# A memset moved behind three weight loads, the first eighth of a written instruction list put in a new order, and seven PSUM evictions on another engine

## The chip, the core and the metric

The kernel runs on one core of a Trainium2 chip. A core has TensorE (PE; its weight loads are shown as PEld), VectorE (DVE), ScalarE (ACT), GpSimd (POOL) and SyncE (SP), each with an in-order queue of its own, an on-chip memory (SBUF) and eight accumulator banks per partition (PSUM), into which only TensorE's products go. Transfers run on 16 DMA engines and are issued from SP, ACT or POOL. The metric is device time in microseconds (us) of one execution; lower is better.

## What is computed

Two stages follow each other. `q`, `k` and `v` have the shape (8, 8, 576, 64) (batch, head, token, dimension), `phi` has (8, 8, 576, 32); all inputs and the output are float32, the kernel computes on float16 operands with float32 accumulation.

```
a    = softmax(phi, over the 32 memory slots)
k_m  = einsum('bhsm,bhsd->bhmd', a, k);  v_m = einsum('bhsm,bhsd->bhmd', a, v)
attn = softmax(q @ k_m^T / 8);           o   = attn @ v_m
x    = o as (4608 tokens, 512)
out  = ((x @ w_a) * (x @ w_b)) @ w_out        # 512 -> 1536 -> 512
```

## The kernel before

**Work.** The eight batches go through the same steps. For a batch, phi is exponentiated (`exp_phi`, L301, ScalarE, in two halves `exp0` and `exp1` of two head pairs each); TensorE forms the sums over tokens of keys, values and a constant column that gives the softmax's denominator (batch 0: `sums`, L387, result pk, one half of the heads at a time; later batches: `kv_sums`, L333, result pkv); VectorE divides them (L396 and L397 for batch 0, `take_kv` L360 and L365 for the others); TensorE turns them (`transpose` L405, `kv_transpose` L373) and VectorE copies them back (L408, L374, the tile kvT, for batch 0 kept in vsum). VectorE turns the queries in 32x32 blocks (`q_transpose` L310, `q_transpose_half` L316). TensorE forms the scores (pscore, L422 and L452), ScalarE their exponentials E (L435, L465). A product with a block matrix of ones (pD, L475) gives the denominators; ScalarE takes Ln (L476) and Exp of its negative (L486), and a tensor_tensor (L240) multiplies into A, the normalised weights.

Instead of forming o, the kernel folds v_m into the weights: `fold` (L526, result pva) multiplies v_m by a slice of w_a or w_b, and `take_fold` (L558) casts the result from PSUM to the float16 tile vab. For batch 0 the first 512 columns are folded in halves of 256. The up-projections (`up_half`, L737) then multiply vab by A: pa is evicted to SBUF as a_sb (L741), pb is multiplied by a_sb on VectorE into ht (L744). Each is done for a batch, a block i of 128 of the 1536 hidden units, and one part of the tokens (288 tokens, for batch 1 320 or 256). The down-projection (L664 and the lines behind it) uses a seven-product scheme on 2x2 blocks, for which sums of tokens (h_sums, from ht) and of weights (w_sums) are formed (L240). From batch 5 on the up-projections use it too (L760).

**What sets the order.** A scheduler doesn't: the string `PLAN` lists every step, and each engine gets its instructions in that order. The letters that matter here: `wa0:256` issues the load of those columns of w_a on GpSimd's queue, and `k1`, `v1`, `p1`, `q1`, `o3` those of keys, values, phi and queries of a batch or a part of w_out; `M` is GpSimd's memset of the constant 1/16 into the tile of keys and values of the odd batches (L802); `O` makes the matrix of ones (memset on VectorE, L269, then two selects on GpSimd, L270 and L272); `F4` runs four matmuls of a zero tile as fill (pw, L229); `0ks1`, `0kt1`, `0vs1`, `0vt1` are the sums of keys or values and their turn for batch 0 and half 1; `0qt1` turns a query block; `0s1`, `0e1`, `0den11`, `0nr11` are scores, exponentials, denominators and normalisation; `0hv0b` and `0hx0b1` are a fold in halves and its cast, `0v1a` and `0x1a0` those of full width; `a1.2.0` and `b1.2.0` are the two up-projections of batch 1, block 2, token part 0; `h0.3` and `g0.3` are a sum of tokens on GpSimd or on VectorE, `T20` and `V00` a sum of weights on GpSimd or VectorE; `d3` takes three steps of the down-projection.

PSUM banks are handed out in order of last use; a fold, scores or pkv hold theirs until their eviction stands in the list. So a TensorE instruction can wait for the eviction, on VectorE or ScalarE, of what its bank held eight allocations earlier.

**Before the list.** The keys of batch 0 come as float32 in two halves, issued from SP and ACT (L185), and VectorE casts them (L235) behind a memset of its own (L233). GpSimd issues phi, queries and values of batch 0 (L149, L160, L155), then makes the identity for the transposes, then takes up the list.

**Which engine evicts.** In `up_half` ScalarE copies every pa. In `take_fold` the two halves g of a fold go to `first` and `second`: VectorE where true, ScalarE where false:

```
first, second = b == 0 and hi <= 512, b < 2
copies = [nc.vector.tensor_copy if x else nc.scalar.copy for x in (first, second)]
```

Of the kernel before, what the change touches and what calls it, by code (L numbers as in the profile page):

```python
# [22 lines left out]
1x1a0 1v0b F1 1x0b0 a0.4.0 1v0a 1x0a0 1qh10 a0.6.1 F1 a0.6.0 1qh00 1x0a1 1qh20 1sh0 1eh10 1eh00 1x0b1 wb512:1024 0v1b  # L23
0x1b0 1x1a1 q1.1 wb1024:1536 wa1024:1536 0x1b1 1v1b a0.5.1 1x1b1 1den10 1den00 b0.6.0 b0.5.1 o3 b0.4.0 1nr10 1nr00
a0.4.1 b0.4.1 a0.7.0 b0.6.1 1qh31 o4 a0.5.0 b0.5.0 1qh01 o0 1x1b0 1qh11 o1 a0.7.1 b0.7.1 a1.3.0 a1.2.0 b1.2.0 o2 o5
a1.1.0 1qh21 a1.4.0 h0.3 b0.7.0 a1.0.0 b1.4.0 1sh1 1eh01 p2 b1.3.0 1eh11 b1.1.0 1v2a 1x2a0 0v2a 1x2a1 0v2b 0x2b0 0x2a1
0x2a0 0x2b1 a1.6.0 k2 b1.6.0 a1.7.0 b1.7.0 a1.5.0 b1.0.0 a1.11.0 a0.10.0 b0.10.0 v2 b1.5.0 p3 1v2b 1x2b0 q2 1x2b1
1den01 a0.8.0 b0.8.0 a0.9.0 b0.9.0 a0.11.1 b0.11.1 1den11 a0.11.0 b0.11.0 T20 1nr01 v3 1nr11 V00 T10 g0.0 a0.10.1
a1.9.0 a0.9.1 b1.9.0 b1.11.0 d3 b0.9.1 d1 b0.10.1 2exp0 a1.8.0 b1.8.0 d1 a0.8.1 d1 a1.5.1 b1.5.1 a1.0.1 b0.8.1 a1.10.0
b1.10.0 a1.11.1 b1.11.1 T21 b1.0.1 a1.6.1 g0.1 a1.4.1 b1.4.1 d1 k3 a1.7.1 V01 b1.6.1 a1.10.1 a1.2.1 b1.2.1 V11 2exp1  # L30
g0.2 a1.1.1 a1.3.1 T31 d2 g1.0 d4 2kv 2km1 d5 2km0 T30 b1.3.1 a1.9.1 d9 q3 2kvt 3exp0 d1 3exp1 b1.1.1 d2 2v1b 2v0a
2x1b0 d1 2qt2 d1 2qt1 p5 g1.1 h1.2 a1.8.1 2qt3 2x0a1 2qt0 d2 2x1b1 d2 2x0a0 d7 q4 d5 2sc d2 2e1 2e0 d2 g2.0 d5 g2.1 d2
b1.8.1 2den1 2den0 b1.9.1 d4 2v1a h1.3 2nr1 2v2b 2x2b1 3kv 2x2b0 d2 3km0 2nr0 3km1 2x1a0 d6 2x1a1 d7 b1.7.1 2v2a v5
2x2a0 2v0b 3qt2 2x0b0 2x0b1 b1.10.1 d2 g2.2 a2.0.0 a2.6.0 b2.6.0 d1 k5 3qt3 2x2a1 d3 3qt1 a2.7.0 a2.2.0 b2.0.0 a2.4.0
d6 v4 d2 3kvt 5exp0 b2.7.0 d2 3qt0 d4 a2.3.0 b2.2.0 3sc 3e0 d2 b2.3.0 3e1 d6 3den0 3nr0 g2.3 a2.1.0 d3 b2.4.0 d3
b2.1.0 a2.5.0 b2.5.0 a2.5.1 a2.8.0 p4 d3 a2.1.1 d3 5exp1 3den1 g4.3 d1 b2.1.1 b2.8.0 a2.9.0 d1 k4 d1 a2.10.1 b2.9.0
# [44 lines left out]
def kernel(  # L81
# [11 lines left out]
    nc = tc.nc  # L93

    B, H, S, D = q.shape
    M = phi.shape[3]
# [194 lines left out]
    def units(b):  # L291
# [3 lines left out]
        u = {}  # L295
# [254 lines left out]
            out, in0, in1 = ((T1, B12, B11), (T2, B22, T1), (T3, B22, B12), (T4, B21, T2))[y]  # L550
            tt(engine, out=out, in0=in0, in1=in1, op=ALU.subtract)

        def take_fold(lo, hi, z, gs=range(2)):
            first, second = b == 0 and hi <= 512, b < 2
            copies = [nc.vector.tensor_copy if x else nc.scalar.copy for x in (first, second)]
            for g, engine_copy in zip(gs, copies[gs[0]:]):
                pva, bank = t["pva", lo, z][g]
                engine_copy(out=vabs[b][z][:, g, lo:hi], in_=pva[:, 0:hi - lo])  # L558
                banks.free(bank)

        def one(f, *a):
            return lambda: f(*a)

        for z in range(2):
            u[f"exp{z}"] = one(exp_phi, z)
            u[f"ps{z}"] = one(slot_sums, z)
            u[f"ks{z}"] = one(sums, z, 0)
            u[f"kt{z}"] = one(transpose, z, 0)
            u[f"vs{z}"] = one(sums, z, 1)
            u[f"vt{z}"] = one(transpose, z, 1)  # L570
            u[f"s{z}"] = one(scores, (z,))
            u[f"e{z}"] = one(exp_scores, z)
            u[f"km{z}"] = one(take_kv, (z,))
            u[f"den{z}"] = one(denominators, z)
            u[f"nr{z}"] = one(normalise, z)
            u[f"sh{z}"] = one(scores_half, z)
            for hf in range(2):
                u[f"eh{z}{hf}"] = one(exp_scores_half, z, hf)
            for hp in range(4):
                u[f"qh{hp}{z}"] = one(q_transpose_half, hp, z)  # L580
            for hf in range(2):
                u[f"den{z}{hf}"] = one(denominators, z, (hf,))
                u[f"nr{z}{hf}"] = one(normalise, z, slice(hf, hf + 1))
            for n in range(NCH):
                for y in range(4):
                    u[f"S{y}{n}{'PD'[z]}"] = one(v_sum, n, y, (nc.gpsimd, nc.vector)[z])
                u[f"v{n}{'ab'[z]}"] = one(fold, 512 * n, 512 * (n + 1), (z,))
                u[f"x{n}{'ab'[z]}"] = one(take_fold, 512 * n, 512 * (n + 1), z)
                for g in range(2):
                    u[f"x{n}{'ab'[z]}{g}"] = one(take_fold, 512 * n, 512 * (n + 1), z, range(g, g + 1))  # L590
            for n in range(2):
                u[f"hv{n}{'ab'[z]}"] = one(fold, 256 * n, 256 * (n + 1), (z,))
                u[f"hx{n}{'ab'[z]}"] = one(take_fold, 256 * n, 256 * (n + 1), z)
                for g in range(2):
                    u[f"hx{n}{'ab'[z]}{g}"] = one(take_fold, 256 * n, 256 * (n + 1), z, range(g, g + 1))
# [133 lines left out]

    a_sbs = {}  # L730

    def up_half(b, i, hf, x):
        ts = tokens(b, hf)
        n = ts.stop - ts.start
        ps = banks.tile([P, n], F32, name=("pa", "pb")[x])
        for g in range(2):
            nc.tensor.matmul(ps, vabs[b][x][:, g, P * i:P * (i + 1)], attn[b][:, g, ts],  # L737
                             start=(g == 0), stop=(g == 1))
        if x == 0:
            a_sbs[b, i, hf] = apool.tile([P, EARLY], F16, name="a_sb")  # L740
            nc.scalar.copy(out=a_sbs[b, i, hf][:, :n], in_=ps)  # L741
        else:
            t0 = S * (b % 2) + ts.start
            nc.vector.tensor_tensor(out=ht[:, i, t0:t0 + n], in0=a_sbs.pop((b, i, hf))[:, :n], in1=ps, op=ALU.mult)  # L744

    sevens = {}

    def seven(k, b, i):
# [6 lines left out]
        x = sevens.setdefault((b, i), {})  # L755
# [6 lines left out]

        def copy(name, po):
            x[name] = upool.tile([P, HALF], F32, name=name)
            nc.scalar.copy(out=x[name], in_=po)  # L765

        def plus(name, po, y):
            x[name] = upool.tile([P, HALF], F16, name=name)
# [26 lines left out]
    for x in PLAN.split():  # L795
        arg = x[1:]
        if x[0] in "fF":
            fill(int(arg), P if x[0] == "f" else 512)
        elif x == "O":
            fill_ones()  # L800
        elif x == "M":
            nc.gpsimd.memset(kv_sbs[1][:, 2], 1.0 / CS)  # L802
        elif x[0] in "wopkvq":
            issue(x)
        elif x[0] in "abu":
            b, i, *hf = (int(y) for y in arg.split("."))
            for h in hf or (0, 1):
                for y in (0, 1):
                    if x[0] in ("u", "ab"[y]):
                        up_half(b, i, h, y)  # L810
        elif x[0] in "PHJ":
            b, i, *z = (int(y) for y in arg.split("."))
            seven(z[0] if z else 8 + "HJ".index(x[0]), b, i)
# [38 lines left out]
```

## Time and profile before

| | us |
|---|---|
| median of three runs | 234.26 |
| lowest and highest | 233.49, 234.87 |
| the profiled execution | 234.62 |
| its span in the trace | 232.8 |
| busy: TensorE | 215.0 |
| busy: VectorE | 195.9 |
| busy: ScalarE | 170.6 |
| busy: GpSimd | 149.7 |

The profile is of one execution. A row of the timeline has start, duration, engine, line, operation, output and inputs with shapes, and a count where neighbours are merged; in brackets it has how long the engine stood idle before it and what released it. A row of the stage table has a stretch, its length, and each engine's busy time with its count of instructions, then the granted TensorE clock, the mean share of the DMA engines and what they moved. A group's row has the count, the busy total, the mean duration in ns and the idle time before. Matmuls overlap, so TensorE counts as busy while its last results drain.

### The profile page before, as it was taken

What the parts mean: (1) busy time and instruction counts of PE and PEld (TensorE: products, weight loads), DVE (VectorE), ACT (ScalarE), POOL (GpSimd) and SP (SyncE); (2) the same over time, 40 slices, a digit from 0 to 9 for tenths busy, and PEclk for the clock granted to TensorE, in tenths of its full rate; (3) what the DMA queues carried; (4) which work ended last, traced back from release to release, by engine and by line L of the source; (5) the groups of instructions that cost most, each with busy time, mean ns of one, the idle gap of its engine ahead of it and who ended that gap; (6) DMA issues with size and microseconds to landing.
All of it is one profiled execution on the core that took longest, in us unless ns stands there. A gap on an engine that the chain in (4) does not pass through costs nothing.

```text
span 232.8 us, 7496 instructions
## 1 busy us (share of the span) xinstructions
PE 215.0 (92%) x2906; PEld 163.9 (70%) x2906; DVE 195.9 (84%) x508; ACT 170.6 (73%) x450; POOL 149.7 (64%) x148
## 2 busy tenths in 40 slices
PE   0469989999999999999999999999999999999992
PEld 0232637688777877876877787887788868888882
DVE  3845789999967766899897999998999999999962
ACT  2216669997899998688897988877898669766330
POOL 7908433954974479995848499599484982772201
PEclk9999999999999999999999999999999999999999
DMA  6999999999999999299936723021403213123063
GB/s 225 241 198 257 205 205 206 218 248 257 207 286 202 224 273 267 40 264 219 207 62 134 127 67 70 23 69 26 93 3 90 65 27 93 26 69 75 23 160 107
DMA packets 26259, 34.09 MB, mean 146 GB/s; under 512 B 2000, under 2 KB 20304, under 8 KB 26224
## 3 DMA queue, kind: packets, MB, share of 16 engines
q0 software_dynamic: 19760, 23.14, 53.9%
q1 hardware_dynamic: 5952, 9.70, 15.7%
q10 hardware_dynamic: 512, 0.79, 1.0%
q8 instruction: 22, 0.36, 0.6%
q14 instruction: 13, 0.11, 0.1%
HBM read 42.47 MB, written 9.44 MB: 223 GB/s over the span
## 4 chain that ended last, share of the span: by engine, by line
PE 91%; DMA 3%; DVE 2%; issue 1%; ACT 0%; POOL 0%; POOLq 0%
PE py L664 21%; PE pa L737 16%; PE pb L737 15%; PE pv L664 10%; PE pva L526 6%; PE py L760 5%; PE px L664 5%; DMA phi_sb<-in_phi_dram 3%; PE pv L760 3%; PE pkv L333 2%; PE pw L229 2%; PE pscore L422 2%; PE pk L387 1%; PE px L760 1%; PE pD L475 1%
## 5 line engine op out<-in xcount | busy, mean ns | idle before, releaser
L744 DVE TENSOR_TENSOR ht<-a_sb,pb 128x288 f16<-128x288 f16 (+2 forms) x144 | 60.5, 445 | 11.1 <-ACT a_sb L741 3.0
L741 ACT CAST a_sb<-pa 128x288 f16<-128x288 f32 (+2 forms) x144 | 55.4, 412 | 14.9 <-PE pa L737 11.0
L737 PEld LDWEIGHTS <-vab 128*128 128x128 f16 x576 | 55.2, 98 | 14.7 <-issue 2.3
L737 PE MATMUL pb<-A,vab 128*128 128x288 f16 (+2 forms) x288 | 55.5, 286 | 0.0
L737 PE MATMUL pa<-A,vab 128*128 128x288 f16 (+2 forms) x288 | 55.1, 286 | 0.1
L558 ACT CAST vab<-pva 128x512 f16<-128x512 f32 x82 | 45.6, 611 | 3.2 <-PE pva L526 3.0
L664 PEld LDWEIGHTS <-h_sums 128*128 128x128 f16 x432 | 41.3, 98 | 9.1 <-issue 2.0
L240 POOL TENSOR_TENSOR h_sums<-ht 128x768 f16<-128x768 f16 x18 | 29.4, 1639 | 11.5 <-DVE ht L744 7.4
L664 PEld LDWEIGHTS <-ht 128*128 128x128 f16 x324 | 31.3, 98 | 7.1 <-issue 1.8
L664 PE MATMUL py<-w_sums,h_sums 128*128 128x256 f16 x216 | 35.5, 273 | 0.0
L664 PE MATMUL pv<-wo_sb,h_sums 128*128 128x256 f16 x216 | 34.3, 273 | 0.0
L765 ACT COPY z<-py 128x288 f32<-128x288 f32 x48 | 19.4, 417 | 6.2 <-PE py L760 4.9
L240 POOL TENSOR_TENSOR ht<-ah,bh 128x288 f16<-128x288 f16 x20 | 14.3, 728 | 11.6 <-DVE ah L769 8.4
L664 PE MATMUL py<-wo_sb,ht 128*128 128x256 f16 x108 | 18.4, 273 | 0.0
L664 PE MATMUL px<-wo_sb,ht 128*128 128x256 f16 x108 | 18.3, 273 | 0.0
L671 ACT ACTIVATE u<-py 128x256 f32<-128x256 f32 x36 | 14.8, 410 | 4.3 <-PE py L664 3.8
L664 PE MATMUL py<-w_sums,ht 128*128 128x256 f16 x108 | 17.8, 273 | 0.0
L435 ACT ACTIVATE E<-pscore 128x288 f16<-128x288 f32 x28 | 9.7, 428 | 8.2 <-PE pscore L422 8.0
L301 ACT ACTIVATE exp_sb<-phi_sb 128x576 f16<-128x576 f32 x16 | 10.9, 700 | 5.7 <-DMA phi_sb<-in_phi_dram 5.7
L240 POOL TENSOR_TENSOR h_sums<-ht,h_sums 128x768 f16<-128x768 f16 x9 | 14.8, 1643 | 0.2
L240 POOL TENSOR_TENSOR h_sums<-h_sums,ht 128x768 f16<-128x768 f16 x7 | 11.5, 1641 | 3.1 <-DVE h_sums L240 2.7
L760 PE MATMUL py<-asum,vab 128*128 128x288 f16 x48 | 13.1, 286 | 0.0
(106 smaller groups left out, 397.8 us busy)
## 6 DMA issues: line engine op xcount, KB each, us to landing
out_dram<-o_sb SPq DMA_DIRECT2D x68, 128.0 KB, 2.4
phi_sb<-in_phi_dram POOLq DMA_DIRECT2D x8, 576.0 KB, 8.5
kv_sb<-in_v_dram POOLq DMA_DIRECT2D x8, 576.0 KB, 12.2
kv_sb<-in_k_dram POOLq DMA_DIRECT2D x7, 576.0 KB, 10.0
q_sb<-in_q_dram POOLq DMA_DIRECT2D x6, 576.0 KB, 8.8
wo_sb<-in_moe_w_out_dram POOLq DMA_DIRECT2D x6, 256.0 KB, 14.1
wa_sb<-in_moe_w_a_dram POOLq DMA_DIRECT2D x2, 512.0 KB, 16.4
wb_sb<-in_moe_w_b_dram POOLq DMA_DIRECT2D x2, 512.0 KB, 13.2
```

What stands on the lines that cost most here:

```text
L240: x = engine.tensor_tensor(**operands)
L301: nc.scalar.activation(out=t["exp"][:, 2 * z:2 * z + 2, :, :], in_=phis[b][:, 2 * z:2 * z + 2, :].rearrange("p c (i m) -> p c i m", m=M), ...
L435: nc.scalar.activation(out=Ev[:, g, :, z, :], in_=pss, func=AF.Exp, scale=1.0 / (8.0 * CS))
L526: nc.tensor.matmul(t["pva", lo, z][g][0][32 * j:32 * j + 32, 0:hi - lo], t["kvT"][64 * r:64 * r + 64, 4 + g if side else 2, M * j:M * j + ...
L558: engine_copy(out=vabs[b][z][:, g, lo:hi], in_=pva[:, 0:hi - lo])
L664: nc.tensor.matmul(po, lhs[:, i], rhs[:, i], start=first and i == 0, stop=i == KH - 1, skip_group_check=not first)
L671: nc.scalar.mul(out=x, in_=po, mul=scale)
L737: nc.tensor.matmul(ps, vabs[b][x][:, g, P * i:P * (i + 1)], attn[b][:, g, ts], start=(g == 0), stop=(g == 1))
L741: nc.scalar.copy(out=a_sbs[b, i, hf][:, :n], in_=ps)
L744: nc.vector.tensor_tensor(out=ht[:, i, t0:t0 + n], in0=a_sbs.pop((b, i, hf))[:, :n], in1=ps, op=ALU.mult)
L760: nc.tensor.matmul(x[bank][0], lhs, rhs, start=first, stop=True, skip_group_check=True)
L765: nc.scalar.copy(out=x[name], in_=po)
```

## The change

1. `M` stands behind the first three weight loads (`wa0:256`, `wb0:256`, `wa256:512`); before, it stood behind the first. `O` comes directly behind it and ahead of the fourth load; before, it stood behind the fourth load, phi and values of batch 1.
2. Two fills and one more stand at the very front of the list. The keys of half 1 are summed first. Turns, sums, denominators, normalisation, folds and early up-projections of batch 0 and the steps of batches 1 and 2 stand in a new order, down to a point shortly before `b1.7.1 2v2a`; from there on the two lists are the same. The later loads in that part change places with neighbours (w_a before w_b in the last third; the order of w_out, `k2` and `k3`).
3. The new letter `c` is an up-projection `a` whose pa is copied by VectorE: `c0.1.0`, `c0.3.0`, `c0.0.0`, `c0.10.0` and `c1.9.1` take the place of the same `a`. The new unit `y` is a cast of a fold with the engine exchanged: `1y2b1` on ScalarE, `2y2b0` on VectorE.
4. Two sums of tokens go from GpSimd to VectorE (`h0.3` and `h1.2` become `g0.3` and `g1.2`) and one goes the other way (`g2.1` becomes `h2.1`).

The products on TensorE are the same, and so is the number of fills. The letter `Q` and the parameter of `seven` are new and not used by the list.

```diff
-0qt1 0exp0 wa256:512 0ks0 F2 0exp1 M 0qt0 wb0:256 wa0:256 0kt0 0s0 wb256:512 0ks1 0kt1 0vs0 0vs1 0qt3 p1 0qt2 0s1 0e0
-0vt0 v1 0e1 O k1 0vt1 0hv1a 0den11 0hx1a0 0nr11 0hx1a1 0den10 0nr10 0den00 0nr00 0hv0a 0hx0a1 wa512:1024 0den01 0hx0a0
-0nr01 F1 0hv1b 0hx1b1 F4 0hx1b0 0hv0b 0hx0b1 a0.0.0 a0.1.1 a0.3.1 0hx0b0 b0.0.0 1exp1 a0.2.0 b0.2.0 b0.1.1 a0.1.0
-b0.1.0 a0.0.1 a0.2.1 b0.3.1 b0.2.1 b0.0.1 1exp0 1kv 1km1 1km0 a0.3.0 b0.3.0 1kvt 0v1a 0x1a0 0x1a1 q1.0 1qh30 1v1a
...
+0exp1 F2 wa0:256 wb0:256 wa256:512 F1 M 0ks1 O 0qt1 0kt1 0qt0 wb256:512 0exp0 0ks0 0kt0 0s0 0e0 0qt3 0qt2 0s1 0e1
+0den00 p1 0vs0 0den01 0nr00 0den11 0nr11 0den10 0nr10 F1 0vs1 0nr01 0vt0 0vt1 0hv0b 0hx0b0 0hv1a 0hv1b 0hx1b0 0hx1b1
+v1 0hx0b1 0hv0a 0hx1a1 F4 0hx1a0 a0.3.1 1exp1 0hx0a1 a0.2.1 0hx0a0 a0.0.1 b0.0.1 c0.1.0 1exp0 b0.2.1 c0.3.0 b0.3.1
+b0.3.0 b0.1.0 c0.0.0 a0.2.0 b0.2.0 b0.0.0 a0.1.1 k1 1kv 1km1 F1 1km0 b0.1.1 1kvt wa512:1024 0v1a 0x1a1 0x1a0 q1.0
...
-        def take_fold(lo, hi, z, gs=range(2)):
-            first, second = b == 0 and hi <= 512, b < 2
+        def take_fold(lo, hi, z, gs=range(2), other=False):
+            first, second = (x != other for x in (b == 0 and hi <= 512, b < 2))
...
+                    u[f"y{n}{'ab'[z]}{g}"] = one(take_fold, 512 * n, 512 * (n + 1), z, range(g, g + 1), True)
...
-    def up_half(b, i, hf, x):
+    def up_half(b, i, hf, x, engine_copy=nc.scalar.copy):
...
-            nc.scalar.copy(out=a_sbs[b, i, hf][:, :n], in_=ps)
+            engine_copy(out=a_sbs[b, i, hf][:, :n], in_=ps)
...
+        elif x[0] == "c":
+            up_half(*(int(y) for y in arg.split(".")), 0, nc.vector.tensor_copy)
```

More of the change, by code (lines that the diff above doesn't have):

```diff
@@ L24 @@
[L24 to L33, printed above, removed]
@@ new lines @@
+a1.4.0 1qh11 a1.1.0 o1 b0.5.1 b1.1.0 a1.0.0 1sh1 1eh01 o4 1eh11 b1.3.0 b1.4.0 o5 0v2a 0x2a0 0x2a1 o2 0v2b a1.6.0 0x2b1
+a1.5.0 b1.5.0 0x2b0 1v2a k2 1x2a1 p2 1v2b 1y2b1 a1.7.0 v2 1x2b0 g0.3 b1.6.0 1x2a0 p3 b1.0.0 a0.11.0 c0.10.0 d2 b1.7.0
+a0.8.0 b0.8.0 q2 1den01 b0.10.0 b0.11.0 a0.11.1 b0.11.1 T20 1nr01 1den11 V00 a1.9.0 1nr11 a0.9.0 b0.9.0 g0.0 d1
+a0.10.1 a0.8.1 a1.11.0 b0.10.1 d1 b1.11.0 a1.5.1 b1.9.0 b1.5.1 b0.8.1 a1.11.1 T10 b1.11.1 d2 T21 a1.10.0 a1.8.0 k3
+a0.9.1 v3 b1.8.0 b1.10.0 a1.0.1 b1.0.1 2exp0 a1.6.1 b0.9.1 a1.2.1 V01 a1.1.1 b1.6.1 g0.1 a1.4.1 a1.7.1 b1.4.1 2exp1
@@ L37 @@
+d3 b2.1.0 a2.5.0 b2.5.0 a2.5.1 a2.8.0 p4 d3 a2.1.1 d3 5exp1 3den1 g4.3 d1 b2.1.1 b2.8.0 a2.9.0 d1 k4 d1 a2.10.1 b2.9.0
 a2.4.1 q5 b2.10.1 3nr1 4qt2 3v0b 3v0a 3x0a0 3x0b0 5kv p6 h3.3 b2.5.1 a2.10.0 3x0a1 d2 a2.11.0 a2.9.1 d2 b2.10.0 d1
@@ L746, with seven @@
     sevens = {}
-    def seven(k, b, i):
+    def seven(k, b, i, engine_copy=nc.scalar.copy):
         n, c = divmod(i, 4)
@@ L764, in copy @@
             x[name] = upool.tile([P, HALF], F32, name=name)
-            nc.scalar.copy(out=x[name], in_=po)
+            engine_copy(out=x[name], in_=po)
         def plus(name, po, y):
@@ L810 @@
                         up_half(b, i, h, y)
-        elif x[0] in "PHJ":
+        elif x[0] in "PQHJ":
             b, i, *z = (int(y) for y in arg.split("."))
-            seven(z[0] if z else 8 + "HJ".index(x[0]), b, i)
+            seven(z[0] if z else 8 + "HJ".index(x[0]), b, i, nc.vector.tensor_copy if x[0] == "Q" else nc.scalar.copy)
         elif x[0] in "TV":
```

12 lines of the change are left out of this document (8 added, 4 removed).

## The prediction

> **What bounds the kernel now.** I read the page first, then a table of busy time by stage, then the timeline of the first 37 us.
>
> ```profile
> PE 91%; DMA 3%; DVE 2%; issue 1%; ACT 0%; POOL 0%; POOLq 0%
> ```
>
> TensorE carries 91% of the chain that ended last. The question is where it still waits. By stage (columns: length, then PE, PEld, DVE, ACT, POOL busy, granted clock, DMA share, GB/s):
>
> ```profile
> 9.12:23.88 14.76, 11.87 (x244) 5.21 (x244) 7.45 (x27) 5.02 (x13) 8.10 (x13) 1.00 1.28 224
> 23.88:36.04 12.16, 10.61 (x208) 5.84 (x200) 9.81 (x28) 8.59 (x23) 4.59 (x7) 1.00 1.28 205
> 36.04:63.00 26.96, 26.96 (x369) 20.38 (x381) 26.40 (x72) 23.48 (x66) 17.68 (x16) 1.00 1.20 229
> 63.00:69.00 6.00, 6.00 (x159) 4.83 (x142) 4.23 (x12) 6.00 (x18) 4.64 (x5) 1.00 1.15 271
> ```
>
> From 36.04 on TensorE has no gap, with VectorE at 26.40 of 26.96 close behind. The list is the same from about 69 us on, and both lists issue the same matrix work before that. So whatever the change gains or loses at 36 us should arrive at the end unchanged, unless VectorE gives way between 36 and 63. The head decides, and it is a chain, not a load.
>
> **The change part by part.** First the memset of ones (L802).
>
> ```profile
> 5.76 2.04 POOL L802 MEMSET kv_sb<- 128x2304 f16 x1
> 5.82 2.60 DVE L235 CAST kv_sb<-ht 128x1152 f16<-128x1152 f32 x1 [2.41 <-DMA ht<-in_k_dram]
> ...
> 8.35 0.94 DVE L235 CAST kv_sb<-ht 128x1152 f16<-128x1152 f32 x1
> 8.38 1.26 ACT L301 ACTIVATE exp_sb<-phi_sb 128x576 f16<-128x576 f32 x2 [5.75 <-DMA phi_sb<-in_phi_dram]
> 9.12 1.15 PE L387 MATMUL pk<-kv_sb,exp_sb 64*32 64x128 f16 x36 [9.12 <-ACT exp_sb L301]
> 10.20 1.04 PE L229 MATMUL pw<-warm 128*128 128x512 f16 x2
> ```
>
> The same cast takes 2.60 us beside the memset and 0.94 without it, so the move frees 1.66 us of VectorE. But pk waited for exp_sb, and that for phi, landed at 8.38; the casts were done at 8.42 (first half, the one pk needs) and 9.29. Phi's issue is not moved. So pk still starts at 9.12: worth 0. The list now begins with the second half (exp1, ks1), which needs both casts: 5.82 + 2 x 0.94 = 7.7, under 9.0. The two loads put ahead of the memset take 0.71 us or more each (the load at 26.73, below), so it starts at 7.2 or later, about when the casts end.
>
> Next the chain up to the first up-projection (pa).
>
> ```profile
> 10.53 0.28 DVE L397 TENSOR_SCALAR kvm<-pk,rphi 128x64 f16<-128x64 f32 x1
> 10.73 0.47 DVE L310 STREAM_TRANSPOSE qT<-q_sb 128x288 f32<-128x288 f32 x1
> 11.39 0.41 PE L405 MATMUL pT<-ident,kvm 128*32 128x128 f16 x8
> 11.84 0.29 DVE L408 COPY vsum<-pT 128x256 f16<-128x256 f16 x1 [0.65 <-PE pT L405]
> ...
> 17.00 0.68 PE L422 MATMUL pscore<-qT,vsum 32*32 32x288 f16 x16 [1.13 <-DVE qT L310]
> 17.72 0.71 ACT L435 ACTIVATE E<-pscore 128x288 f16<-128x288 f32 x2 [4.11 <-PE pscore L422]
> 19.15 0.90 PE L475 MATMUL pD<-E,ones 128*128 128x288 f16 x3 [0.28 <-POOL ones L272]
> 19.61 0.41 ACT L476 ACTIVATE asum<-pD 128x288 f32<-128x288 f32 x1 [1.18 <-PE pD L475]
> 21.23 0.41 PE L526 MATMUL pva<-wb_sb,vsum 64*32 64x256 f16 x8
> 21.58 1.89 PE L229 MATMUL pw<-warm 128*128 128x512 f16 x4
> 22.37 0.44 ACT L486 ACTIVATE vsum<-asum 128x288 f16<-128x288 f32 x1
> 23.18 1.59 DVE L558 CAST vab<-pva 128x256 f16<-128x256 f32 x4
> 23.88 0.91 PE L737 MATMUL pa<-A,vab 128*128 128x288 f16 x6
> ```
>
> Before, two fills (1.04) stood between pk and pT, and the second E ended at 18.43. In the new order pT follows pk at once: kvm 10.81, pT 10.87 to 11.28; the second pk (1.15) to 12.37; its kvm to 12.91, pT to 13.38, copy to 13.71; scores of group 0 to 14.44; two transposes (0.83) end at 14.55, scores of group 1 at 15.28; E done at 16.02: 2.4 us earlier. The matrix of ones (L269 to L272) now stands ahead of those transposes on VectorE and behind the memset on GpSimd, done before 12; the 0.28 us wait of pD goes.
>
> What is late next: eight Ln and Exp on ScalarE, 3.2 us together (19.61 to 22.81), run from 16.05 to 19.2. On VectorE three normalises, each behind its Exp, stand in front of the kvm of the second value sum; it waits in that queue until 19.1 though its matmuls end at 17.6. After it: transpose (half of 0.41), the last normalise, two copies (0.2 each, an estimate from the larger one's 0.29), fold at 20.05. Four folds step by 0.35 (21.23 to 21.58), then four fills of 0.42 ((1.89 - 1.04) / 2) end at 23.2. VectorE starts the eight casts of 0.40 at 20.55, loses 0.2 to the second fold, ends the sixth (the last that the first pa reads) at 23.2 and the eighth at 23.98. So pa starts at 23.25 instead of 23.88: 0.63 gained.
>
> Then the stretch where three of eight copies of pa move to VectorE.
>
> ```profile
> 24.33 1.00 ACT L741 CAST a_sb<-pa 128x288 f16<-128x288 f32 x3 [1.52 <-PE pa L737]
> 25.20 0.71 ACT L301 ACTIVATE exp_sb<-phi_sb 128x576 f16<-128x576 f32 x1
> 25.36 0.45 DVE L744 TENSOR_TENSOR ht<-a_sb,pb 128x288 f16<-128x288 f16 x1 [0.59 <-ACT a_sb L741]
> 26.23 2.28 DVE L744 TENSOR_TENSOR ht<-a_sb,pb 128x288 f16<-128x288 f16 x6 [0.42 <-PE pa L737]
> 26.73 0.71 POOL L178 DMA_DIRECT2D wo_sb<-in_moe_w_out_dram  x1 [1.77 <-DMA kv_sb<-in_k_dram]
> 28.18 0.94 PE L333 MATMUL pkv<-kv_sb,exp_sb 64*32 64x192 f16 x72 [0.48 <-DVE ht L744]
> 29.18 0.17 DVE L360 RECIPROCAL rphi<-pkv 128x1 f32<-128x1 f32 x1 [0.68 <-PE pkv L333]
> 30.91 0.36 DVE L374 COPY kvT<-pT 128x384 f16<-128x384 f16 x1
> 31.32 0.41 PE L526 MATMUL pva<-wa_sb,kvT 64*32 64x512 f16 x8
> 34.61 0.89 ACT L465 ACTIVATE E<-pscore 128x160 f16<-128x160 f32 x4
> 35.76 0.43 PE L475 MATMUL pD<-E,ones 128*128 128x320 f16 x2
> 36.04 0.91 PE L737 MATMUL pb<-A,vab 128*128 128x288 f16 x6
> ```
>
> ```profile
> L558 ACT CAST vab<-pva 128x512 f16<-128x512 f32 x82 | 45.6, 611 | 3.2 <-PE pva L526 3.0
> ...
> L558 DVE CAST vab<-pva 128x512 f16<-128x512 f32 x10 | 6.4, 678 | 0.5 <-PE pva L526 0.5
> L558 DVE CAST vab<-pva 128x256 f16<-128x256 f32 x2 | 0.8, 418 | 0.1
> L240 DVE TENSOR_TENSOR h_sums<-ht,h_sums 128x768 f16<-128x768 f16 x2 | 1.1, 545 | 0.0
> ```
>
> The trace has no cast of 288 columns on VectorE. Between the two casts above it would last 0.45, a step of 0.43; the bounds are 0.38, the step of the products (2.28 / 6), and 0.68. I take 0.43, nearest to the 256 row. From pa at 23.25 ScalarE is free at 23.7: a copy (1.00 / 3), the exp of the next phi (0.71), then two copies, of which the second (0.40) is the one that the first product reads: 25.45, against 25.36 before. So VectorE, free from 23.98, idles 1.5 us and then has ten operations where it had seven in front of the reciprocal: 7 x 0.38 + 3 x 0.43 = 3.95, to 29.43. The key sums (pkv) wait for the bank of the sixth of them, 27.95 to 28.9, so they no longer decide; their keys had landed by 26.73 at the latest, before and after. Reciprocal at 29.45 instead of 29.18: the 0.63 is gone and 0.27 lost. The same 2.1 us follow to kvT and the next folds (31.6 for 31.32). ScalarE then has four casts of 512 (0.61 by the row, a step of 0.55 where neighbours overlap) and three copies of pa from 31.7 to 34.95, E (0.89) to 35.85, pD at 35.9; in the new order the last pa of this group stands behind pD and not in front, 0.25 more (its two matmuls of 0.125). The dense stage starts at 36.40 for 36.04: **0.36 us later**.
>
> Behind it, up to 69 us: VectorE gets one cast of 288 and one of 256 (0.45 + 0.42), two sums of tokens come from GpSimd and one goes back (+0.55), and the casts 1x2b1 and 2x2b0 trade places with ScalarE (0.68 off, 0.68 on). Net 1.4 us against 26.96 - 26.40 = 0.56 us idle up to 63 and 1.8 us idle from 63 to 69. I cost it at nothing, since the banks let VectorE lag and its work may slip behind 63; if that cover is gone it costs 0.9 to 1.4.
>
> Queues: GpSimd issues two weight loads 2 us earlier; the fourth, phi and values of batch 1 about 2 us later (they stand behind the memset and behind ones, which waits for VectorE until 11.0); the keys of batch 1 and what follows earlier. The DMA row of 9.12 to 36.04 shows the queues full (share over 1), so the data come in the order of issue and the end of the line stays: worth 0; if the fourth weight load did come 2 us later, the fold that reads it could lose some tenths. Later loads only change places with neighbours. The three fills moved to the front run while TensorE waits for phi anyway. SP's queue isn't touched.
>
> **Sum:** 0 + (-0.63) + 0.90 (25.45 and ten operations in place of seven) + 0.09 = +0.36 us. The profiled execution took 234.62 us (span 232.8 and 1.8 around it), 0.36 above the median of 234.26; on the median this gives 234.6.
>
> **The rivals.** *The lead survives.* VectorE idles 1.5 us in my reckoning; if ScalarE gives the first copies sooner, or the moved casts take 0.38, the head keeps its 0.63, and the key sums may start as early as their data, 26.8 for 28.18: 1.4. For it: ScalarE loses 1.05 us of copies there. Against: two exps and one VectorE queue. 234.26 - 0.6 to 1.4 = 232.9 to 233.6.
>
> *VectorE becomes the bound* (the other side). Place: 36 to 63, where it is 98% busy. The mechanism decides once its lag exceeds the eight PSUM banks; from then each of the 1.4 us holds TensorE. With the 0.36 of the head: 235.5 to 236.0. Against: GpSimd and the products are moved as well, and with VectorE at 98% TensorE shows no gap there.
>
> *The memset still meets a cast.* The second cast is now what pk needs. If the memset starts at 7.3, the last 0.4 us of work drags on beside it (2.0 us of overlap did about 0.32 us of work: 0.94 less the 0.62 left at 7.80), to 9.4: pk 0.3 later, 234.9.
>
> *TensorE's clock.* The granted clock reads 1.00 throughout, yet the fills at 21.58 take 0.42 per 512 columns, and pa at 23.88 at most 0.15 per 288 (0.91 / 6), 0.27 per 512: TensorE went from about half pace to full pace near 23.5. In the new order TensorE idles between 17.6 and 20.05. If the half pace lasts through the fifteen half products, they take 30 x 0.24 = 7.1 us, to 30.35, pkv ends at 31.3, and the reciprocal comes 1.9 us later than forecast: 236.5. [...]
>
> **How the numbers follow.** A measurement tells about 0.5% (1.2 us) from no change. Forecast 234.6, own range 233.9 to 235.3: 0.44. Lead survives: 0.24, about half of it below 233.1. VectorE bound: 0.18, nearly all above 235.4. Memset meets a cast: 0.06. Clock: 0.08. Hence faster 0.15, same 0.60, slower 0.25. The range takes in the lower part of the first rival and all of the second: 233.1 to 236.2.
>
> **What would show it.** Casts of L235 both near 0.94 and pk still at 9.1; pD with no wait for ones; pa near 23.3; VectorE idle for over a microsecond behind the eight casts of vab; the reciprocal near 29.4; TensorE without gaps from about 36.4. I am wrong if pa starts after 23.9 or before 22.5 (chain of Exps misread), if the reciprocal comes before 28.5 (lead kept), or if TensorE shows waits for VectorE between 36 and 63.

## The result and the profile after

The changed kernel takes 236.86 us (median of six runs, 236.09 to 237.53) against 234.14 us (233.49 to 234.87) before: a ratio of 1.0116, 95% interval 1.0089 to 1.0142. It is slower, by more than the range on record allowed. The profiled execution took 236.62 us with a span of 234.7, so 2.0 us more than that of before and 1.9 more in span.

The page of the changed kernel gives the chain that ended last, by engine:

```profile
PE 84%; DVE 9%; ACT 2%; DMA 2%; issue 1%; DVEq 0%
```

TensorE carried 91% of it before and VectorE 2%, so some part of the chain has passed to VectorE. The stage table of the changed kernel, in the columns of the prediction's, says where TensorE lost work:

```profile
9.12:23.88 14.76, 9.81 (x241) 5.04 (x241) 8.39 (x28) 4.29 (x12) 8.71 (x13) 0.97 1.28 223
23.88:36.04 12.16, 10.97 (x195) 6.42 (x196) 10.35 (x31) 6.78 (x19) 4.06 (x6) 0.89 1.28 205
36.04:63.00 26.96, 26.13 (x340) 19.06 (x339) 26.21 (x69) 22.49 (x64) 15.44 (x15) 1.00 1.20 229
```

Two places: the first stage (TensorE 9.81 us busy where it had 11.87, of which 1.04 are the two fills behind pk that now run before 9.12), and the third, which had no gap before (26.96 of 26.96) and now has one of 0.83 us, although VectorE is busy there for 0.2 us less than before. The timeline of the changed kernel's head (start, duration, engine, line):

```profile
5.76 0.75 POOL L174 DMA_DIRECT2D wb_sb<-in_moe_w_b_dram  x1
5.79 2.07 DVE L235 CAST kv_sb<-ht 128x1152 f16<-128x1152 f32 x1 [2.38 <-DMA ht<-in_k_dram]
6.49 0.76 POOL L174 DMA_DIRECT2D wa_sb<-in_moe_w_a_dram  x1
7.22 2.59 POOL L803 MEMSET kv_sb<- 128x2304 f16 x1
7.78 2.65 DVE L235 CAST kv_sb<-ht 128x1152 f16<-128x1152 f32 x1
...
10.57 1.15 PE L387 MATMUL pk<-kv_sb,exp_sb 64*32 64x128 f16 x36 [7.84 <-DVE one_cs L276]
...
21.28 0.52 PE L526 MATMUL pva<-wb_sb,vsum 64*32 64x256 f16 x8
21.86 2.74 DVE L558 CAST vab<-pva 128x256 f16<-128x256 f32 x8 [0.41 <-PE pva L526]
24.00 1.62 PE L738 MATMUL pa<-A,vab 128*128 128x288 f16 x6 [0.43 <-DVE vab L558]
26.30 0.45 DVE L745 TENSOR_TENSOR ht<-a_sb,pb 128x288 f16<-128x288 f16 x1 [1.70 <-ACT a_sb L742]
29.96 0.17 DVE L360 RECIPROCAL rphi<-pkv 128x1 f32<-128x1 f32 x1
36.64 0.66 PE L738 MATMUL pb<-A,vab 128*128 128x288 f16 x4
```

The two casts of the keys end at 7.86 and 10.43 where they ended at 8.42 and 9.29, and pk, which waits for VectorE (for the small memset of one_cs that stands behind the casts in its queue) and no longer for phi's exponentials, starts 1.45 us later. That nearly all of this is caught up by pa, at 24.00, is the new order at work. The second place is the turn to batch 2. The changed kernel:

```profile
57.18 0.55 DVE L240 TENSOR_TENSOR h_sums<-ht,h_sums 128x768 f16<-128x768 f16 x1
57.41 3.73 POOL L240 TENSOR_TENSOR w_sums<-wo_sb,w_sums 128x768 f16<-128x768 f16 x2 [1.73 <-DVE w_sums L240]
57.65 2.00 DVE L240 TENSOR_TENSOR h_sums<-ht 128x768 f16<-128x768 f16 x1
59.57 0.15 DVE L360 RECIPROCAL rphi<-pkv 128x1 f32<-128x1 f32 x1
60.82 0.42 PE L373 MATMUL pT<-ident,rep 128*128 128x128 f16 x3 [0.83 <-DVE rep L365]
```

The kernel before, at the same steps:

```profile
57.02 0.55 DVE L240 TENSOR_TENSOR h_sums<-ht 128x768 f16<-128x768 f16 x1
57.20 3.48 POOL L240 TENSOR_TENSOR w_sums<-wo_sb,w_sums 128x768 f16<-128x768 f16 x2 [3.14 <-DVE h_sums L240]
57.49 0.16 DVE L360 RECIPROCAL rphi<-pkv 128x1 f32<-128x1 f32 x1
59.20 0.33 PE L373 MATMUL pT<-ident,rep 128*128 128x128 f16 x3
```

The same sum of tokens takes 0.55 us when GpSimd's sum starts behind it, and 2.00 when GpSimd's sum has begun 0.24 us before it: 1.45 us, about one GpSimd sum (half of 3.48) less the 0.24 us that it had already run. The reciprocal and the turn pT stand behind it on VectorE's queue, and TensorE waits 0.83 us. The lag behind the kernel before, in the two profiled executions, beside the forecast's:

| | before | after | lag | forecast |
|---|---|---|---|---|
| first sums of keys (pk) | 9.12 | 10.57 | +1.45 | 0 |
| first up-projection (pa) | 23.88 | 24.00 | +0.12 | -0.63 |
| reciprocal, batch 1 | 29.18 | 29.96 | +0.78 | +0.27 |
| dense stage | 36.04 | 36.64 | +0.60 | +0.36 |
| turn pT, batch 2 | 59.20 | 60.82 | +1.62 | +0.36 |
| end of the span | 232.8 | 234.7 | +1.9 | +0.36 |

These are single executions, and they differ from one to the next. Phi's exponentials start anywhere from 7.73 to 8.38 in the fourteen profiled executions of this case. The changed kernel and the kernel of the experiment "T30 behind the token sum" have the same list up to 36 us, and from pk to pa they took 13.43 and 13.93. So a lag in the head is known to about 0.6 us.

### The profile page after: what moved, and what is told of

Same layout as the page of the kernel before. It is cut to its first block, busy times and chain, and to the rows that moved or that the text cites. A ratio compares the mean times of both kernels' runs of the same rounds, so it can differ in the third digit from the quotient of the medians.

```text
span 234.7 us, 7495 instructions
## 1 busy us (share of the span) xinstructions
PE 216.0 (92%) x2906; PEld 164.6 (70%) x2906; DVE 199.3 (85%) x514; ACT 168.8 (72%) x445; POOL 148.3 (63%) x147
## 4 chain that ended last, share of the span: by engine, by line
PE 84%; DVE 9%; ACT 2%; DMA 2%; issue 1%; DVEq 0%
PE py L665 20%; PE pb L738 14%; PE pa L738 14%; PE pv L665 10%; PE pva L526 5%; PE py L761 5%; PE px L665 5%; PE pv L761 3%; DMA ht<-in_k_dram 2%; DVE kv_sb L235 2%; PE pkv L333 2%; DVE vab L558 1%; PE pscore L422 1%; DVE ht L745 1%; PE px L761 1%; PE pk L387 1%
## 5 line engine op out<-in xcount | busy, mean ns | idle before, releaser
L738 PEld LDWEIGHTS <-vab 128*128 128x128 f16 x576 | 55.9, 99 | 16.2 <-issue 2.2
L742 ACT CAST a_sb<-pa 128x288 f16<-128x288 f32 (+2 forms) x139 | 53.9, 416 | 18.5 <-PE pa L738 15.3
L240 POOL TENSOR_TENSOR h_sums<-ht 128x768 f16<-128x768 f16 x17 | 27.7, 1642 | 8.1 <-DVE ht L745 3.7
L240 POOL TENSOR_TENSOR h_sums<-h_sums,ht 128x768 f16<-128x768 f16 x8 | 13.1, 1640 | 3.1 <-DVE h_sums L240 2.7
L240 POOL TENSOR_TENSOR h_sums<-ht,h_sums 128x768 f16<-128x768 f16 x8 | 13.1, 1643 | 0.2
```

The lines of the kernel that those rows point to most:

```text
L240: x = engine.tensor_tensor(**operands)
L742: engine_copy(out=a_sbs[b, i, hf][:, :n], in_=ps)
```

## The experiments

**The theory** after the result: both losses are one thing. VectorE's float32 cast of the keys in SBUF (2.65 us beside the memset, 0.94 in the kernel before), or its sum of two SBUF tiles (2.00 us where GpSimd's sum had begun, 0.55 ahead of it), and an instruction of GpSimd (memset, sum, the issue of a load) take turns, whole instructions at a time. Held this way, the memset put behind the loads costs the head and `T30` ahead of `g1.0` costs the turn to batch 2. **The rivals:** the time went with the seven evictions and the sums moved to VectorE, or with the chain's new order and the lower clock of TensorE (0.89 in the second stage above). The next four kernels have twelve executions each, beside 35 of the kernel before, which took 234.84 us there.

**The memset behind ones.** In the new list, behind the two selects that wait for VectorE:

```diff
- F1 M 0ks1 O 0qt1
+ F1 0ks1 O M 0qt1
```

> The changed kernel with the one edit that GpSimd's memset stands behind the two selects that make the matrix of ones, which wait for VectorE, and so behind both casts of the first keys. Theory A (a cast on VectorE and an instruction of GpSimd take turns at SBUF, so that the second cast in the changed kernel waited for the end of the memset at 9.81 us and pk came at 10.57): first cast about 2.0 us, second about 0.6, pk near 8.6, the first up-projection near 22.5, the dense stage at 36.0 or earlier; time 1.0 to 1.5 us below the changed kernel, ratio to the kernel before 1.005 to 1.008. Rival B (the evictions and sums moved to VectorE are the loss, the head is ruled by the chain of Ln and Exp and by data): pk may come early, but the dense stage still begins near 36.6 and the ratio stays at 1.010 to 1.013.

Measured: 234.9 us, ratio to before 1.0006 [0.9981, 1.0031], so by the ratios about 1.1% under the changed kernel. Its timeline:

```profile
5.77 1.11 POOL L174 DMA_DIRECT2D wb_sb<-in_moe_w_b_dram  x1
5.81 0.76 DVE L235 CAST kv_sb<-ht 128x1152 f16<-128x1152 f32 x1 [2.40 <-DMA ht<-in_k_dram]
6.49 0.95 DVE L235 CAST kv_sb<-ht 128x1152 f16<-128x1152 f32 x1
6.87 0.87 POOL L174 DMA_DIRECT2D wa_sb<-in_moe_w_a_dram  x1
33.57 0.41 PE L526 MATMUL pva<-wb_sb,vsum 64*32 64x512 f16 x8 [0.51 <-DMA wb_sb<-in_moe_w_b_dram]
55.74 2.00 DVE L240 TENSOR_TENSOR h_sums<-ht 128x768 f16<-128x768 f16 x1
```

The casts are done at 7.44 instead of 10.43, pk starts at 8.57 behind phi's exponentials and the dense stage at 34.74, 1.9 us earlier than in the changed kernel. The order of the steps and the evictions are those of the changed kernel, so neither is what cost the time in the head. The stall of 2.00 us in the second place is still there. The gain was more than expected; what stops it short is new: the fold at 33.57 waits for its weights.

**T30 behind the token sum.** One token of the list moved, so that GpSimd's sum of weights is issued behind VectorE's `g1.0`:

```diff
- V11 T30 d6 2kv d1 g0.2 d2 T31 g1.0 d3 2km1 2km0 d8
+ V11 d6 2kv d1 g0.2 d2 T31 g1.0 d3 2km1 2km0 T30 d8
```

> The changed kernel with the one edit that GpSimd's sum of weights T30 stands behind the sums of tokens g0.2 and g1.0 and the division of batch 2, as in the kernel before. Theory A (in the changed kernel T30 ran beside VectorE's sum of tokens g1.0, which took 2.00 us for 0.55 and held the division of batch 2's keys, so that TensorE stood still for 0.83 us before 60.82): g1.0 takes 0.55 to 0.6, the gap in front of the turn of batch 2 is gone, time 0.9 to 1.2 us below the changed kernel, ratio 1.006 to 1.008. Rival B (VectorE has more work than it can do up to 63 us, whichever instruction it is that runs late): the wait moves elsewhere, the ratio stays at 1.010 to 1.013.

Measured: 235.8 us, ratio 1.0039 [1.0015, 1.0063], somewhat below the ratio that was expected. Its timeline and its row of the stage table:

```profile
58.31 0.55 DVE L240 TENSOR_TENSOR h_sums<-ht 128x768 f16<-128x768 f16 x1
60.48 0.33 PE L373 MATMUL pT<-ident,rep 128*128 128x128 f16 x3
```

```profile
36.04:63.00 26.96, 26.96 (x352) 19.81 (x352) 26.03 (x71) 23.23 (x67) 14.60 (x14) 1.00 1.20 228
```

The sum is back at 0.55 us, TensorE has no gap from 36 to 63, and every eviction and sum that the change gave VectorE is still on it. So the gap was one stall, not VectorE's load.

**Both repairs.**

> The changed kernel with both edits: memset behind the matrix of ones, T30 behind the sums of tokens. Theory A: both losses are the whole loss, and they add: pk near 8.6, no wait at 60 us, time 2.0 to 2.7 us below the changed kernel, ratio 0.997 to 1.003. Rival B: ratio above 1.006. A third outcome: the earlier head leads on, and the ratio is below 0.995.

Measured: 233.96 us, ratio 0.996 [0.9935, 0.9985]: below the changed kernel, and 0.4% below the kernel before. The profiled execution of this kernel is the longest of its twelve (235.11 us). The medians of the spans show that the two losses add: 234.8 us for the changed kernel (six runs), 232.9 with the memset behind ones (-1.9), 233.8 with T30 moved (-1.0), 231.7 with both (-3.1), twelve runs each, and 232.7 for the kernel before on the chip of the last three.

**The memset alone, in the old list.** The kernel before, with `M` behind the three loads:

```diff
- 0exp1 M 0qt0 wb0:256 wa0:256
+ 0exp1 0qt0 wb0:256 wa0:256 M
```

> The kernel before with the one edit that the memset stands behind three weight loads instead of one; the rest of the list is the old one. Theory A: the casts take about 2.0 and 2.65 us and end near 10.4 as in the changed kernel, but the old list begins with the half whose keys are cast first, so pk still starts near 9.1; the division behind it waits for VectorE until 10.5 for 10.3; ratio 0.999 to 1.002. Rival C (it is the memset's place by itself, whatever the list, that costs the 1.4 us of the head): pk near 10.5, ratio 1.005 or more.

Measured: 235.1 us, ratio 1.0013 [0.9985, 1.004]. Its timeline:

```profile
5.73 2.14 DVE L235 CAST kv_sb<-ht 128x1152 f16<-128x1152 f32 x1 [2.32 <-DMA ht<-in_k_dram]
7.23 2.58 POOL L802 MEMSET kv_sb<- 128x2304 f16 x1
7.79 2.65 DVE L235 CAST kv_sb<-ht 128x1152 f16<-128x1152 f32 x1
```

The casts are held as in the changed kernel, to 7.87 and 10.44, and it costs nothing: the old list sums the first half of the keys first, which needs only the first cast, and pk starts at 8.80 behind phi's exponentials. The late memset costs only together with the new list's `0ks1` at the front, which needs both casts.

**The memset ahead of the loads**, in the new list (for this kernel and the next three, the kernel before took 234.46 us):

```diff
- F2 wa0:256 wb0:256 wa256:512 F1 M
+ F2 M wa0:256 wb0:256 wa256:512 F1
```

> The changed kernel with the memset of the constant ahead of all three weight loads. Turn theory (a cast of the keys takes turns with whole GpSimd instructions, the writing of a load's descriptors included): the memset runs from about 5.0 to 7.1 us and holds the first cast until then, so that it shows about 1.8 us and ends at 7.7; the second cast waits for the weight load that GpSimd took up meanwhile and ends at 8.4 to 9.3. pk then starts between 8.6 (where phi's exponentials let it) and 9.4, at least a microsecond ahead of the 10.57 of the changed kernel, and the time is 234.7 to 235.6 us, 0.993 to 0.997 of the changed kernel, since the loss near 57 us stays. Rival (only the memset holds a cast, a load never does): the second cast ends at 8.3 and pk stands at 8.6 in any case. Rival (the early loads are what matters, not the casts): the loads land 2 us later, the folds near 21 us wait for them, and the time is no better than that of the changed kernel, 236.9.

Measured: 234.6 us, ratio 1.0003 [0.9988, 1.0019]. Its timeline:

```profile
4.99 2.02 POOL L803 MEMSET kv_sb<- 128x2304 f16 x1
5.62 1.99 DVE L235 CAST kv_sb<-ht 128x1152 f16<-128x1152 f32 x1 [2.21 <-DMA ht<-in_k_dram]
6.95 0.98 POOL L174 DMA_DIRECT2D wa_sb<-in_moe_w_a_dram  x1
7.54 0.94 DVE L235 CAST kv_sb<-ht 128x1152 f16<-128x1152 f32 x1
```

The first cast ends 0.60 us behind the memset (7.61 and 7.01), the load 0.32 behind the cast (7.93), the second cast 0.55 behind the load (8.48): one after the other, as the theory has it. The three loads are issued 2 us later than in the changed kernel, and no fold that reads them waits: the lead of early loads is worth nothing here.

**The seven evictions back**, on top of both repairs (`c` back to `a` five times, `1y2b1` to `1x2b1`, `2y2b0` to `2x2b0`).

> The changed kernel with both repairs (memset behind ones, T30 behind the token sum), and the seven evictions back on the engines that had them before. Theory (the seven evictions are worth nothing measurable either way): the reciprocal of the second batch's keys comes at 27.6 to 28.3 us against 28.2 with the repairs alone, since seven operations stand on VectorE in place of ten but ScalarE has three more copies; the fold near 33.4 us waits for its weights in any case; 0.994 to 0.999 of the kernel before, within 0.3% of the run with both repairs. Rival, as I had it in the prediction (the three copies on VectorE cost 0.9 us up to the reciprocal): reciprocal at 27.4 or earlier and, where the weights allow it, up to 0.5 us less in all, 0.992 to 0.994. Rival (ScalarE is the scarce engine and the evictions are the gain of the change): reciprocal at 28.6 or later, waits of TensorE for ScalarE between 36 and 63, 0.999 to 1.003.

Measured: 234.03 us, ratio 0.9983 [0.996, 1.0005]. The reciprocal comes at 27.91 instead of 28.23 with a first pa at 22.42 instead of 22.30, so the three early copies cost 0.44 us between the two (in the other kernels with these copies that stretch took 5.70 to 6.11 us, here 5.49); but the fold behind them then waits longer for its weights, and the time is no better:

```profile
33.73 0.41 PE L526 MATMUL pva<-wb_sb,vsum 64*32 64x512 f16 x8 [0.68 <-DMA wb_sb<-in_moe_w_b_dram]
```

**The three sums of tokens back**, on top of both repairs (`g0.3` and `g1.2` to GpSimd, `h2.1` to VectorE).

> The changed kernel with both repairs, and the three sums of tokens back on the engines that had them before: two on GpSimd, one on VectorE. Theory (the sums are worth nothing, VectorE has room between 36 and 63 us): up to 36 us nothing differs; VectorE is busy some 0.5 us less between 36 and 63, TensorE shows no gap there; 0.994 to 0.998 of the kernel before. Rival (VectorE is the bound there, so each sum on it costs): 0.4 to 0.6 us less than with both repairs, 0.992 to 0.994. Rival (a sum on GpSimd takes turns with VectorE's sums, as near 57 us in the changed kernel): a new wait of a VectorE instruction of L240 for over a microsecond beside a GpSimd sum, and 0.5 to 1.5 us more, 0.998 to 1.003.

Measured: 233.58 us, ratio 0.9971 [0.9947, 0.9996]. Not to be told from both repairs alone. TensorE has no gap from 36 to 63 and VectorE is busy for 26.40 us of it, with both repairs alone 26.39: it fills that stage in either case. A new turn of the kind looked for does appear (0.55 us against 1.88), but TensorE shows no gap for it:

```profile
61.45 1.64 POOL L240 TENSOR_TENSOR h_sums<-ht,h_sums 128x768 f16<-128x768 f16 x1 [0.58 <-DVE h_sums L240]
61.62 1.88 DVE L240 TENSOR_TENSOR h_sums<-ht 128x768 f16<-128x768 f16 x1
```

**A shorter chain in the head**, on top of both repairs: the second value sum ahead of two normalises.

```diff
- 0den11 0nr11 0den10 0nr10 F1 0vs1 0nr01 0vt0 0vt1 0hv0b 0hx0b0 0hv1a
+ 0den11 0vs1 0nr11 0vt0 0vt1 0den10 0nr10 F1 0hv0b 0hx0b0 0nr01 0hv1a
```

> The changed kernel with both repairs, and the second sum of values and the turns ahead of two of the normalises: the scaling of that sum waited for 1.8 us in VectorE's queue behind normalises whose exponentials came late. Theory (from 33 us on the data of the weights set the head): the first up-projection starts at 21.3 to 21.9 us in place of 22.3, but the fold of the second half of w_b near 33.4 us still waits for its load, now longer (0.28 before), the dense stage starts at 34.7 to 34.9 as before, and the time is that of both repairs within 0.2%. Rival (the chain of the head still sets it): the dense stage starts 0.5 to 0.9 us earlier, at 34.0 to 34.4, and the time is 0.2 to 0.4% less, 0.992 to 0.994 of the kernel before.

Measured: 233.51 us, ratio 0.9956 [0.994, 0.9972]. The first pa came at 22.08 against 22.30 with both repairs alone, later than expected, but pk started at 9.04 instead of 8.60 in this execution: the chain between them is 0.66 us shorter, and 0.38 shorter than in the run with the sums back (13.43), whose list is the same there. The fold that needs the late weights:

```profile
33.39 0.41 PE L526 MATMUL pva<-wb_sb,vsum 64*32 64x512 f16 x8 [0.50 <-DMA wb_sb<-in_moe_w_b_dram]
```

In the six kernels so far whose casts are free early, this fold starts at 33.39 to 33.73 and waits 0.28 to 0.74 us for its load, and the dense stage starts at 34.65 to 34.91, whether the reciprocal came at 27.91 or at 28.25. The load sets this. When it is issued does not seem to decide: with the memset ahead of the loads it was issued at 16.41, in the run with both repairs at 17.53, and the fold started at 33.48 and 33.44. That the total would move if the load came sooner was not tried.

**Why the first cast waits for two loads.** One thing did not fit. In the changed kernel the first cast waited through two loads, while in the kernels with the memset elsewhere it ran at once and the load waited for it. Four more kernels, variants of the changed kernel with one execution each, take that apart; their traces carry the argument, not their times. First, a memset of two columns of an unused tile in its place, and the large one behind ones:

```diff
- F1 M 0ks1 O 0qt1
+ F1 M 0ks1 O N 0qt1
...
+            nc.gpsimd.memset(tiny, 0.0)
```

> The changed kernel with a memset of two columns of an unused tile in the place of the large memset behind the three weight loads, and the large one behind ones. The turns of whole instructions leave one thing open: with the large memset queued behind the loads the first cast waited for two loads (2.07 us, three kernels of three), with a select that waits for VectorE behind them it ran at once (0.76 us) and the load took longer in its place. Theory Q (a GpSimd instruction on SBUF that is queued without a wait keeps the casts off from before its start, whatever its size): the first cast still starts at 5.7 and ends near 7.86, the second at 8.4 to 8.5 behind the small memset, and pk stands at 8.6 to 9.2. Theory S (the size of the memset is what matters): the casts take 0.76 and 0.95 us, pk at 8.6. Either way pk is over a microsecond ahead of the changed kernel's 10.57, and the one time is 234.0 to 235.6 us.

Measured: 234.75 us (before 234.13).

```profile
5.75 0.76 DVE L235 CAST kv_sb<-ht 128x1152 f16<-128x1152 f32 x1 [2.34 <-DMA ht<-in_k_dram]
6.42 0.95 DVE L235 CAST kv_sb<-ht 128x1152 f16<-128x1152 f32 x1
```

The first cast runs at once, and pk starts at 8.50. So a memset queued there doesn't hold the casts by itself; the size, or the tile written, must matter, and the third and fourth kernel show the size. Second, the fourth weight load ahead of the memset:

```diff
- wa256:512 F1 M 0ks1 O 0qt1 0kt1 0qt0 wb256:512
+ wa256:512 wb256:512 F1 M 0ks1 O 0qt1 0kt1 0qt0
```

> The changed kernel with the fourth weight load, too, ahead of the memset. Theory Q without a limit (a queued memset keeps the casts off however many loads stand in front): the first cast waits for all loads, to 8.6 us, the memset runs to 10.6 and the second cast ends at 11.2, pk at 11.3. Theory Q with a limit (it looks about two instructions ahead): the first cast, which comes when the second load has just begun, runs at once in 0.76 us, the second is held until the end of the last load near 8.2 and ends at 8.8, the memset after it; pk at 8.9. Theory L (the loads themselves hold it, one at a time): the first cast ends at 7.1, the second at 7.9. The one time is 234.5 to 237.5 us.

Measured: 235.27 us. None of the three forms fits both casts:

```profile
5.81 2.13 DVE L235 CAST kv_sb<-ht 128x1152 f16<-128x1152 f32 x1 [2.40 <-DMA ht<-in_k_dram]
7.22 1.02 POOL L174 DMA_DIRECT2D wb_sb<-in_moe_w_b_dram  x1
7.86 0.94 DVE L235 CAST kv_sb<-ht 128x1152 f16<-128x1152 f32 x1
8.23 2.52 POOL L803 MEMSET kv_sb<- 128x2304 f16 x1
```

The first cast ends at 7.94, nearly where it did (7.86), with one load more in front of the memset: the hold ends at a time, not at a place in the queue. Third and fourth, half and three quarters of the memset in its place and the rest behind ones:

```diff
-            nc.gpsimd.memset(kv_sbs[1][:, 2], 1.0 / CS)
+            nc.gpsimd.memset(kv_sbs[1][:, 2, :2], 1.0 / CS)
```

> The changed kernel with half of the memset (1152 columns, about 1.0 us) in its place behind the three weight loads and the other half behind ones. Theory R (a part of GpSimd that is not busy with the loads starts the memset early, from about 5.2 us, and shuts the casts out for the memset's own length; in the changed kernel that end, 5.2 + 2.0, fell by chance on the end of the third load, and with a fourth load ahead of the memset it stayed at 7.3): the first cast is released at 6.2 to 6.3 and ends at 6.8 to 6.9, so that it shows 1.0 to 1.2 us; the second ends at 7.4 to 7.8 or behind the shown memset. Theory T (the casts wait for the end of the third load in any case, when a memset without a wait stands behind it): the first cast ends at 7.86 as in the changed kernel. Theory S (only a memset above some size holds the cast): 0.76 us, end at 6.5. Time 234.3 to 236.0 us.

> The same with three quarters of the memset (1728 columns, about 1.5 us) behind the three loads and a quarter behind ones. Theory R: the first cast is released at 6.7 to 6.8 and ends at 7.3 to 7.4, half a microsecond behind the run with half of the memset. Theory T: 7.86 again. Theory S: either 6.5 or 7.86. Time 234.3 to 236.5 us.

Measured: 234.67 and 234.87 us (before 234.76). With half:

```profile
5.69 1.40 DVE L235 CAST kv_sb<-ht 128x1152 f16<-128x1152 f32 x1 [2.28 <-DMA ht<-in_k_dram]
```

With three quarters:

```profile
5.79 1.59 DVE L235 CAST kv_sb<-ht 128x1152 f16<-128x1152 f32 x1 [2.38 <-DMA ht<-in_k_dram]
7.67 2.04 POOL L803 MEMSET kv_sb<- 128x1728 f16 x1
```

The first cast ends at 7.09, 7.38, 7.86 and 7.94 with half, three quarters, all, and all behind four loads. Taking off the 0.61 us that it needs once it is let in (in the changed kernel, from the third load's end at 7.25 to 7.86), it was let in at 6.48, 6.77, 7.25 and 7.33. From three quarters to all that is 0.48 to 0.56 us, and a quarter of the memset lasts 0.5; the half missed its expectation by 0.2 us and falls on the end of the second load (6.50). So the hold grows with the memset, as if a part of GpSimd began it near 5.25, while the loads were still being issued. No row of the trace shows such an early part, and the row of the memset is none the shorter for it: it ended 0.99, 1.47 and 1.95 us (half, three quarters, all) behind the cast that it met, and alone the half took 1.06 and the whole 2.02. So the early part stays an inference; what is shown is that the size and the place of the memset decide, and that the first cast is held from 1.4 us before the row of the memset begins (5.79 and 7.22).

## Why the prediction was wrong, point by point

**The memset, "worth 0".** This step failed. Its place in the text is the sum for the second half, "5.82 + 2 x 0.94 = 7.7, under 9.0", and "it starts at 7.2 or later, about when the casts end". The memset did start at 7.22. But 0.94 was not a cast left alone: in the row of before the second cast was waiting for the load issued at 7.72, which ended at 8.72, and ended 0.57 us behind it. Nor was the 2.60 a cast slowed by sharing: it ended 0.62 us behind the memset (8.42 and 7.80), as the casts that were let in behind a memset did later (0.60 with the memset ahead of the loads). I took every slowdown to come from the memset and read the loads as free, so the move freed nothing of VectorE: the two casts held it from 5.79 to 10.43, before from 5.82 to 9.29. With the first cast held to 7.86 the memset, next in turn, ran before the second, and pk came 1.45 us late. The rival "The memset still meets a cast" had the mechanism and the cast right, and let the two share the time (0.3 us) where the cast was held to the end of the memset (10.43 and 9.81). Taken against the repaired kernels this step is the larger loss: the span is 1.9 us shorter with the memset behind ones.

**The chain to the first pa, -0.63.** Right in kind: from pk to pa the new order took 13.43 us, against 14.76 before and 14.13 in the forecast (13.43 to 13.95 in the eleven executions with this part of the list, 14.87 in the other one with the old list). The wait of pD for ones went, as said. The casts of vab were over-priced: eight in 2.74 us, a step of 0.34 and not 0.40, so that pa came 2.72 us behind the first fold and not 3.20. The 0.63 was not absent; it was 1.33 in this execution, and 0.8 to 1.4 over all of them, and the casts of the keys took 1.45 back.

**The copies on VectorE, +0.90.** Right in sign, a little too large: pa to reciprocal took 5.96 us against 5.30 before, 0.66 more, and putting the copies back gave 0.44. The idle stretch of VectorE behind the eight casts was 1.70 us (forecast 1.5). The last term, +0.09, was -0.18. The sum itself has a slip: 25.45 and 3.95 give 29.40 and not 29.43.

**The dense stage, +0.36.** It came at +0.60, near the forecast, but as the sum of a first term that was wrong by 1.45 and a second that was wrong by 0.70 the other way: no evidence for the working.

**"I cost it at nothing" from 36 to 69.** This failed too, and is the larger part of what lies between the forecast and the end: +1.02 us at the turn to batch 2, from one sum of tokens held for 1.45. I counted there how much work VectorE was given and not what stood beside it on GpSimd: the new list puts `T30` ahead of `g1.0`. A wait of TensorE for VectorE in this stretch was the last of the prediction's own signs of being wrong. Another 0.3 came between there and the end; no run takes that apart.

**The rivals.** "VectorE becomes the bound" named the place and the side, but not the mechanism: with VectorE's work unchanged and `T30` moved, TensorE has no gap. "The lead survives" describes what the new order does once both stalls are gone: 34.91 against 36.04 at the dense stage, and 0.4% in all. "TensorE's clock" happened in part: six products of the first pa took 1.62 us instead of 0.91, and the granted clock reads 0.89 in that stage, 0.50 from 24 to 26 us. The slow stretch was over by 27 (0.78 from 26 to 27, 1.00 from 27 to 28) and did not last through the fifteen half products, as the rival had it. It cost little: from pa to reciprocal took 5.96 us here and 5.70 with the memset ahead of the loads, where the six took 0.90, so 0.26 us between these two. The reading doesn't show every such stretch: with `T30` moved the six took 1.60 us at a granted clock of 1.00.

**The queues.** "Worth 0" for the later fourth load was right for the changed kernel, but a load, which the prediction read as harmless, is what now stops the repaired head near 33.5 us. In the run with both repairs DMA carries 10% of the chain that ended last, against 3% before. That the full queues make this load late (a share of 1.28, as before) fits the two times of issue above, but is argued and not shown.

## What to carry to other kernels

A duration in a trace is the time of an operation only if nothing held it meanwhile: the casts of the keys, of one shape, took 0.76 to 2.65 us here. Before a row is used as a price, look at what GpSimd did between its start and its end, loads included. When an instruction is moved past others, list for each of its new neighbours which engine pair they form, and price a meeting at the whole of the other instruction, not at a share: here a 0.55 us sum cost 1.45 us more. A part that was worth nothing in the old order (the late memset, 1.0013) made up most of a loss of a per cent in the new one (1.0116, and 1.0006 with the memset behind ones), so the parts of a change are priced in the order that they will meet.

## What the runs showed of the hardware

- The float32 casts of the keys on VectorE and GpSimd's loads went in turn. In eleven executions a load ended 0.30 to 0.32 us behind the cast that it met (with the memset behind ones 6.57 and 6.88; in the kernel before 8.42 and 8.72), and the next cast 0.55 to 0.57 us behind that load. So a load seems to need its turn for its last 0.3 us alone, and a cast for about 0.6 (an estimate from these rows).
- Where GpSimd's memset had begun, such a cast was held to its end: in five executions the cast ended 0.60 to 0.63 us behind it (before 8.42 and 7.80, in the changed kernel 10.43 and 9.81).
- VectorE's sum of two SBUF tiles took 0.55 us where GpSimd's sum began 0.18 us behind its start (57.20 and 57.02 in the kernel before), and 2.00, 1.99 and 1.88 where GpSimd's had begun 0.24, 0.24 and 0.17 us ahead of it (the changed kernel, the memset ahead of the loads, the sums of tokens back). GpSimd's two sums beside it took 3.73 us in the first two of these, for 3.48 in the kernel before. That the engines take turns is read from these rows; what makes them do so is not shown.
- In the changed kernel the first cast was held from 1.4 us before the row of the memset began (5.79 and 7.22), and for a time that grew with the size: it ended at 7.09, 7.38 and 7.86 with half, three quarters and all of the memset. The cause is open.
